# Strassen sums and centring by accumulating transfers in a Mish and convolution kernel

## The chip, the cores and the metric

The kernel runs on one core of one Trainium2 chip. The metric is the device time of one execution in microseconds. The chip executes a program on several engines that each work through a queue of their own in order: PE (matrix products), DVE (vector work), ACT (activations and copies), POOL (GpSimd) and SP, which only issues DMA transfers. Engines meet by semaphores: an instruction at the head of a queue waits until what it needs is done, and everything behind it in that queue waits too.

## The reference

The input `x` has 2048 rows of 640 channels. The output is `x + A(xn) + B(xn)`, where `xn` is `x` after a layer norm over the channels.

```python
xn = (x - mean(x)) / sqrt(var(x) + 1e-5)
h = xn @ w1 + b1                        # 640 -> 1728
act = h * tanh(softplus(h))             # Mish
B = act @ w2                            # 1728 -> 640
A = convolution of xn with K along the rows, + xn * D_skip
K = 2 * Re(sum_n C[d,n] * dt[d] * exp(dt[d] * A[d,n] * l))
```

For parameters as they are given here, `A` is computed as two running sums along the rows with coefficients per channel; a general path stands behind a flag that the kernel computes at run time and that isn't taken.

## The kernel before, in words

**Tiles.** Everything is transposed: channels lie on the 128 partitions, rows of `x` run along the free dimension. The 2048 rows are four blocks b of TB = 512. The 640 channels are KD = 5 tiles k, the 1728 hidden channels NF = 14 tiles f: thirteen of 128 and one, f = 8, of 64. Each operand of a product is split into a high and a low fp16 part, and each product is three: high by high, low by high and high by low. The first product of a tile, `mm1` (L773 in the profile), has 15 matmuls of 128x128x512; the second, `mm2` (L825), has 15 as well and adds into five accumulators ACC in PSUM. `mm2` runs LAG = 3 tiles behind `mm1`.

**Strassen.** In blocks 1 to 3 twelve of the fourteen tiles are taken in six pairs, PAIRS = (0, 2, 4, 6, 9, 11). For a pair, `mm1_pair` (L793) splits the problem two by two: two tiles f, two halves CA and CB of the 512 rows, and the four channel tiles 0 to 3 as two sets, {0, 2} and {1, 3}. It computes seven half-size products where plain work has eight. They are issued as five pieces called one, two, three_a, three_b and four, between which pieces of `mm2` are put. In between, small instructions move partial sums: `cV` and `cY` (ACT, L1029 and L1030) copy PV and PX out of PSUM bank TR, `z` and `w` (DVE, L1033 and L1037) add PVS to PY. Piece two waits for `cY`, three_a for `z`, four for `w`. The fifth channel tile is done plainly. Block 0 uses plain `mm1` for all tiles.

**Sums that Strassen needs.** Of the weights, four sums per pair, made once, in block 0 and block 1: `load_s` (L543) loads both tiles of a pair again from DRAM on SP's queue into two tiles of the pool "w", `sum_w` (L550, L552, L554, L556) makes the four sums of 128x256 on DVE, and `hi_s` (ACT, L568) and `lo_s` (DVE, L572) split them into fp16 parts, in three pieces of 256, 256 and 512 columns. The first sum takes the place of the even channel tiles of W1H[f+1] and W1L[f+1], which only block 0's plain product needs otherwise; the other three go to SWH[i] and SWL[i]. Of `x`, five differences per block, `sum_x` (L583), split by `hi_t` (L586) and `lo_t` (L590) into TH, TL, EH, EL.

**The layer norm of block c** for c = 1 to 3 is done while block c - 1 is computed: SP loads four tiles of rows (`lx`, L1086, pool "x" of two tiles), DVE makes their statistics (L597 to L599), POOL the reciprocal root and a copy of the means (`rstds`, L603, L604, L1193). PE transposes the eight columns (`spread`, L608), ACT copies them out of PSUM (`sr`, L612), SP writes them to DRAM (`sd`, L616) and loads them back, broadcast to all partitions, mean and rstd as two tiles (`spread_l`, L620). SP loads the transposed `x` (`load_xt`, L1189), and DVE subtracts the mean and multiplies by rstd, ten instructions of 128x512 (`norm_t`, L624). Then ACT and DVE split the result (`hi_x`, L535, and `lo_x`, L538), and `sum_x` follows. `spread` stands in PE's queue behind `mm1` of tile 7 in block 0, and in the fourth pair in blocks 1 and 2. Block 0 is normalised ahead of the rest, before its transposes.

**The convolution** of a block and channel tile (`ka` to `ke`, L709 to L729) needs two scans on DVE and ends with `ke`, which turns the tile XT[c][k] into the skip part of the output. POOL then adds `x` from DRAM into a copy of the accumulators with an accumulating DMA (`add_x`, L518), adds that into XT (`finish`, L739) and stores (`store`, L742). In the last block PE's last products and DVE's last sums alternate, and SP stores.

**What sets the order.** The function `whole` adds every piece of work to a planner, class Plan, with its engine, an assumed cost in microseconds, what it needs, which tile of a pool it takes and gives back, and for a DMA its kB. PE's order is fixed by the order of the `add` calls. For all other engines, and SP's and POOL's DMA issues, the planner walks through an assumed time and picks what is ready with the earliest due time; due times follow back from PE's order. `due` in `add` gives soft due times; `edge` spreads the convolution's over the run. The planner's order is the order of each engine's queue; at run time only semaphores count.

Of the kernel before, what the change touches and what calls it, by code (L numbers as in the profile page):

```python
# [20 lines left out]
P = 128  # L21
L = 2048
D = 640
# [10 lines left out]
HALF = 8  # L34
LAG = 3
# [201 lines left out]
def ffn_general(tc, x, xT, vec, w1, w2, out):  # L237
# [3 lines left out]
    with ExitStack() as es:  # L241
# [12 lines left out]
        for b in range(NB):  # L254
# [11 lines left out]
            for f, (n, o) in enumerate(zip(FC, FO)):  # L266
# [5 lines left out]
                for k in range(KD):  # L272
                    pe.matmul(h[:n], W1[:, k, :n], XN[:, k], start=k == 0, stop=k == KD - 1)
# [149 lines left out]
def body(ctx: ExitStack, tc: tile.TileContext, x, xT, logA, Aim, Cr, Ci, logdt, vec, w1, w1T, w2, w2T, out):  # L423
# [64 lines left out]
    XT, ACT, SM, NX = ({} for _ in range(4))  # L488
    NCHK = NF + 3 * KD
# [51 lines left out]
    def load_s(i, j):  # L541
        o = D * FO[PAIRS[i] + j]
        sp.dma_start(kf(pl["sw", i, j]), w1[o:o + D * P].rearrange("(p k f) -> p k f", p=P, k=KD))  # L543

    def sum_w(i, j):

        w = lambda n, m: kf(pl["sw", i, n])[:, 0:4].rearrange("p (q j) f -> p q j f", j=2)[:, :, m]
        t = lambda n: pl["ss", i, n // 2].rearrange("p (j q f) -> p j q f", j=2, q=2)[:, n % 2]
        if j == 0:
            v.tensor_tensor(t(0), w(1, 0), w(1, 1), op=OP.add)  # L550
        elif j == 1:
            v.tensor_tensor(t(1), t(0), w(0, 0), op=OP.subtract)  # L552
        elif j == 2:
            v.tensor_tensor(t(2), w(0, 0), w(1, 0), op=OP.subtract)  # L554
        else:
            v.tensor_tensor(t(3), w(0, 1), t(1), op=OP.subtract)  # L556

    def part_w(i, j):
        f = PAIRS[i] + 1
        t = pl["ss", i, j // 2].rearrange("p (j q f) -> p j q f", j=2, q=2)  # L560
        if j == 0:
            sh, sl = (w[f][:, 0:4].rearrange("p (q j) f -> p q j f", j=2)[:, :, 0] for w in (W1H, W1L))
            return sh, sl, t[:, 0]
        return (SWH[i][:, 0], SWL[i][:, 0], t[:, 1]) if j == 1 else (SWH[i][:, 1:3], SWL[i][:, 1:3], t)
# [12 lines left out]
    def sum_x(c, j):  # L577

        x = XT[c][:, 0:4].rearrange("p (q j) t -> p q j t", j=2)
        b11, b12, b21, b22 = (x[:, :, i, h] for i in range(2) for h in (CA, CB))  # L580
        p, q = ((b12, b11), (b22, j == 1 and stage(c, 0)), (b22, b12), (b21, j == 3 and stage(c, 1)),
                (XT[c][:, 4, CA], XT[c][:, 4, CB]))[j]
        v.tensor_tensor(stage(c, j), p, q, op=OP.subtract)  # L583

    def hi_t(c, j):
        a.activation(EH if j == 4 else TH[j], stage(c, j), AF.Copy, scale=SX)  # L586

    def lo_t(c, j):
        hi, lo = (EH, EL) if j == 4 else (TH[j], TL[j])
        v.scalar_tensor_tensor(lo, stage(c, j), SX, hi, op0=OP.mult, op1=OP.subtract)  # L590
# [27 lines left out]
    def spread_l(c):  # L618
        for j in range(2):
            sp.dma_start(pl["b", c][j], NX["sd"][j * NT:(j + 1) * NT].rearrange("(o i) p -> o (i p)", o=1).to_broadcast([P, TB]))  # L620

    def norm_t(c, k, j):
        z = XT[c][:, k]
        v.tensor_tensor(z, z, pl["b", c][j], op=(OP.subtract, OP.mult)[j])  # L624

# [118 lines left out]
    def bank(b, f):  # L744

        if b > 0:
# [3 lines left out]
    def mm1_part(f, kinds, c, start=False, stop=False, ks=range(KD)):  # L750
# [3 lines left out]
        for j, ((w, x), k) in enumerate(seq):  # L754
            pe.matmul(bank(0, f)[:, c], w[:, k], x[k][:, c], start=start and j == 0, stop=stop and j == len(seq) - 1)  # L755

    def mm1(b, f):
# [3 lines left out]
        hh, lh, hl = ([(h, w[f][:, k], x[k]) for k in range(KD)] for w, x in ((W1H, xh), (W1L, xh), (W1H, xl)))  # L761
# [13 lines left out]
    def mm1_pair(b, f):  # L775

        i = PAIRS.index(f)
        wh = [[W1H[f + j][:, k] for k in range(KD)] for j in range(2)]
        wl = [[W1L[f + j][:, k] for k in range(KD)] for j in range(2)]
# [133 lines left out]
    def whole():  # L913
# [8 lines left out]
        def chain(b, f, pre, drop=()):  # L922
# [7 lines left out]
            elif b > 0 and f in PAIRS:  # L930
# [52 lines left out]
        for f in range(3, NF):  # L983
            prev = {3: 0, 4: 1}.get(f, f - 2)
            add(("m1", 0, f), M, 15 * M5 if FC[f] == P else 1.85, mm1, 0, f,
                pre=[("hw1", f), ("ow1", f), ("v1", 0, prev), ("sg", 0, prev)] if f > 3 else [("v1", 0, prev), ("sg", 0, prev)])
            chain(0, f, [("m1", 0, f)])
            if f == 7:
                add(("spread", 1), M, 0.1, spread, pre=[("rs", 1)])
            for o in second(0, f - LAG, []):  # L990
                o()


        def vc(b):
            return ("vX", b - 1, PAIRS[-1]) if b > 1 else ("v1", 0, 2)

        for b in range(1, NB):
            for f in range(NF):
                n = (b, f)
                if f - 1 in PAIRS:  # L1000
# [3 lines left out]
                if f not in PAIRS:  # L1004
                    pb = before(b, f)
                    add(("m1", *n), M, 15 * M5 if FC[f] == P else 1.85, mm1, b, f,
                        pre=[("v1", b, f - 2), ("sg", b, f - 2)])
                    chain(b, f, [("m1", *n)])
                    for o in second(*g2, []):
# [3 lines left out]
                c = b  # L1013
                one, two, three_a, three_b, four = mm1_pair(b, f)
                p0 = (b, PAIRS[i - 1]) if i else (b - 1, PAIRS[-1])
                first = b == 1 and i == 0
                lastB = ("v1", 0, LAST) if first else ("v1", *before(b, f)) if f in (0, 9) else ("v1", *p0)
                lastC = ("v1", 0, LAST - 1) if first else ("v1", p0[0], p0[1] + 1)
                lastA = [("v1", 0, 2), ("sr", 1)] if first else [("cY", *p0), ("vX", *p0)]
                if (b, i) in ((1, 4), (2, 4), (3, 4)) and b < NB - 1:  # L1020
                    lastA.append(("sr", b + 1))
                if (b, i) == (NB - 1, NP - 1):
                    lastA.append(("oke",))
                SWD = lambda j: [("os", i, j)] if b == 1 else []
                TXD = lambda j: [("tl", b, j)]
                XLD = lambda ks: [("lo", b, k) for k in ks]
                A2, B2 = second(*g2, [9] if FC[g2[1]] == P else [6]), second(*h2, [3, 9] if FC[h2[1]] == P else [2, 6])
                add(("one", *n), M, 12 * M2, one, pre=lastA + SWD(0) + TXD(0) + XLD((0, 2)))
                add(("cV", *n), A, 0.36, lambda: a.copy(PVS, PV), pre=[("one", *n)] + ([] if first else [("w", *p0)]))  # L1029
                add(("cY", *n), A, 0.36, lambda: a.copy(PY, PX), pre=[("cV", *n), lastC])  # L1030
                A2[0]()
                add(("two", *n), M, 15 * M2, two, pre=[("cY", *n)] + SWD(1) + TXD(1) + XLD((1, 3, 4)))
                add(("z", *n), V, 0.38, lambda: v.tensor_tensor(PZ, PY, PVS, op=OP.add), pre=[("two", *n), lastB])  # L1033
# [7 lines left out]
                if i == NP - 2 and b == NB - 1:  # L1041
                    add(("oks",), M, 0.1, ok_sum, pre=[("ce", "last"), ("vX", *n)])
# [7 lines left out]
                chain(b, f + 1, [("four", *n), ("w", *n)])  # L1050

# [30 lines left out]
        for c in range(1, NB):  # L1082
            b = c - 1
            t0 = start(b, 0)
            for i in range(NT):
                add(("lx", c, i), S, 0.1, lambda c=c, i=i: sp.dma_start(pl["x", c, i], xr[c, i]),  # L1086
                    pre=[("st", c, i - 2)] if i > 1 else [], take=("x", ("x", c, i), 1), rel=t0, kb=327.0)
# [4 lines left out]
            add(("bc", c), S, 0.2, spread_l, c, pre=[("sd", c)], take=("b", ("b", c), 2 * KD), kb=512.0)  # L1092
# [260 lines left out]
```

## Time and profile before

| what | us |
|---|---|
| median of 3 runs (360.0 to 360.25) | 360.2 |
| the profiled execution | 359.29 |
| its span, first to last instruction | 357.5 |
| PE busy in the span | 350.6 |
| DVE busy | 311.1 |
| ACT busy | 296.3 |
| POOL busy | 50.4 |
| block 0's `mm1` and `mm2` behind the start, to the first piece of block 1 | 20.7 to 89.2 |
| block 1, 2, 3 begin at | 89.2, 174.1, 258.8 |

The profile is of one execution. Its times are from the span's start. A row of a group gives line, engine, operation, names and shapes, a count, the busy time, the mean duration in ns, and the idle time of that engine just before with what ended it. A row of the timeline gives start, duration and the instruction. A row of the waits says which engine waited for what: total, times, longest. A matmul's duration includes its way through the array; the pace is the distance from one start to the next.

### The profile page before, as it was taken

The page shows a single profiled execution, that of the slowest core. Times are in us where ns is not written, and L with a number is a line of the kernel's source. Part 1 is how long each engine was busy: PE and PEld are TensorE (multiplying, and loading weights), DVE is VectorE, ACT ScalarE, POOL GpSimd, SP SyncE. Part 2 cuts the span into 40 slices and gives each one's busy share as a digit, 9 for nine tenths or more (in the row PEclk, how much of TensorE's full clock was granted, in tenths as well). Part 3 has the DMA queues.
Part 4 walks back from the last instruction along what each step waited for, and adds up shares of the span by engine and source line. Part 5 has one row for each costly group of instructions (what it writes and reads, how often), then busy time and mean ns, then how long its engine had stood idle before and what let it go on. Part 6 is the DMA issues. An engine that isn't in the chain of part 4 may idle for free.

```text
span 357.5 us, 6018 instructions
## 1 busy us (share of the span) xinstructions
PE 350.6 (98%) x2167; PEld 211.5 (59%) x2167; DVE 311.1 (87%) x585; ACT 296.3 (83%) x614; POOL 50.4 (14%) x72
## 2 busy tenths in 40 slices
PE   7999999999999999999999999999999999999995
PEld 6754444444666665665566666566566666566543
DVE  5989989989998999999999986899997888775552
ACT  3599999978488799889989897989978989868740
POOL 2100020000013041000103343000003552000000
PEclk9999999999999999999999999999999999999999
DMA  7879975105109954911256973941111994201003
GB/s 238 279 240 296 337 247 174 73 1 183 39 21 194 335 165 127 296 24 39 64 179 128 202 181 91 278 170 35 33 35 20 166 232 89 55 0 31 0 16 141
DMA packets 26036, 48.75 MB, mean 136 GB/s; under 512 B 3576, under 2 KB 6928, under 8 KB 26000
## 3 DMA queue, kind: packets, MB, share of 16 engines
q1 hardware_dynamic: 19152, 34.21, 29.8%
q0 software_dynamic: 6240, 13.11, 17.8%
q10 hardware_dynamic: 608, 0.98, 0.8%
q8 instruction: 19, 0.31, 0.4%
q14 instruction: 17, 0.14, 0.2%
HBM read 39.10 MB, written 5.26 MB: 124 GB/s over the span
## 4 chain that ended last, share of the span: by engine, by line
PE 95%; DMA 1%; DVE 1%; SPq 0%; ACT 0%; issue 0%; DVEq 0%
PE acc L825 48%; PE h L793 18%; PE h L773 14%; PE tr L793 12%; DMA x<-in_A_u_dram 1%; PE h L755 1%; PE tr L755 1%; PE acc L1217 0%; PE acc L839 0%; PE acc L836 0%; PE acc L837 0%; DVE w1l L526 0%; DVE st L598 0%; SPq L1236 0%; DVE st L597 0%
## 5 line engine op out<-in xcount | busy, mean ns | idle before, releaser
L825 PE MATMUL acc<-hi,w2h 128*128 128x512 f16 x273 | 100.9, 379 | 0.0
L825 PE MATMUL acc<-hi,w2l 128*128 128x512 f16 (+1 forms) x265 | 99.7, 379 | 0.0
L825 PE MATMUL acc<-lo,w2h 128*128 128x512 f16 x253 | 93.3, 379 | 0.0
L825 PEld LDWEIGHTS <-w2h 128*128 128x128 f16 x526 | 51.2, 98 | 48.4 <-issue 1.3
L863 ACT ACTIVATE s<-h,cv 128x512 f32<-128x512 f32 (+1 forms) x51 | 30.9, 605 | 23.6 <-PE h L793 18.4
L793 PEld LDWEIGHTS <-w1h 128*128 128x128 f16 x432 | 42.3, 98 | 10.7
L887 DVE SCALAR_TENSOR_TENSOR A<-p,A 128x512 f32<-128x512 f32 (+1 forms) x56 | 38.2, 682 | 7.2 <-ACT p L882 7.0
L825 PEld LDWEIGHTS <-w2l 128*128 128x128 f16 x273 | 25.6, 98 | 30.7 <-issue 1.1
L872 ACT ACTIVATE p<-s,kc 128x512 f32<-128x512 f32 (+1 forms) x56 | 40.1, 715 | 0.5
L882 ACT ACTIVATE p<-p,kc 128x512 f32<-128x512 f32 (+1 forms) x56 | 40.0, 714 | 0.2
L877 ACT ACTIVATE p<-p,kc 128x512 f32<-128x512 f32 (+1 forms) x56 | 39.9, 713 | 0.2
L905 DVE SCALAR_TENSOR_TENSOR lo<-A,hi 128x512 f16<-128x512 f32 x52 | 35.3, 680 | 3.6 <-ACT hi L894 3.3
L867 DVE SCALAR_TENSOR_TENSOR A<-h,bs,s 128x512 f32<-128x512 f32 (+1 forms) x51 | 33.0, 647 | 6.2 <-ACT s L863 6.0
L894 ACT ACTIVATE hi<-A 128x512 f16<-128x512 f32 (+1 forms) x56 | 34.9, 624 | 3.6 <-DVE A L887 3.4
L518 POOL DMA_DIRECT2D r<-in_xT_dram x15 | 13.7, 1094 | 126.8 <-ACT r L736 60.3
L773 PEld LDWEIGHTS <-w1h 128*128 128x128 f16 (+1 forms) x174 | 15.3, 99 | 20.3 <-issue 3.3
L715 DVE TENSOR_TENSOR_SCAN g<-g,car,kc 128x512 f32<-128x512 f32 x20 | 25.6, 1278 | 1.1 <-ACT g L709 1.1
L793 PEld LDWEIGHTS <-w1l 128*128 128x128 f16 x216 | 21.1, 98 | 8.4 <-issue 0.3
L719 DVE TENSOR_TENSOR_SCAN g<-g,car,g 128x512 f32<-128x512 f32 x20 | 25.5, 1276 | 0.1
L793 PE MATMUL tr<-xh,w1h 128*128 128x256 f16 x90 | 24.5, 273 | 0.1
L793 PE MATMUL tr<-xl,w1h 128*128 128x256 f16 x90 | 24.5, 273 | 0.0
L793 PE MATMUL tr<-xh,w1l 128*128 128x256 f16 x90 | 24.5, 273 | 0.0
(174 smaller groups left out, 728.7 us busy)
## 6 DMA issues: line engine op xcount, KB each, us to landing
w<-in_w_dram SPq DMA_DIRECT2D x23, 320.0 KB, 4.7
w<-in_w2T_dram SPq DMA_DIRECT2D x15, 288.0 KB, 6.4
w<-in_B_w_dram SPq DMA_DIRECT2D x13, 320.0 KB, 3.5
w<-in_w1T_dram SPq DMA_DIRECT2D x13, 320.0 KB, 6.6
x<-in_A_u_dram SPq DMA_DIRECT2D x12, 320.0 KB, 5.0
xt<-in_xT_dram SPq DMA_DIRECT2D x15, 256.0 KB, 5.5
r<-in_xT_dram POOLq DMA_DIRECT2D x15, 256.0 KB, 6.0
xt<-r POOLq DMA_DIRECT2D x15, 256.0 KB, 4.1
```

The costliest lines, as they stand in the source:

```text
L715: v.tensor_tensor_scan(g1[:, 1:], g1[:, 1:], zero.to_broadcast([P, TB]), car[:, 1, k:k + 1], op0=OP.add, op1=OP.add)
L773: pe.matmul(o, w, x, start=(j == 0), stop=(j == len(order) - 1))
L793: pe.matmul(o, p, q, start=start and n == 1, stop=n == 3 * len(w), skip_group_check=True)
L825: pe.matmul(o, w, x, start=start, stop=stop)
L863: a.activation(pl["s", b, f][:n, c], src(b, f) if h is None else h, AF.Sigmoid, bias=cv[:n, f:f + 1], scale=1 / SH)
L867: v.scalar_tensor_tensor(pl["A", b, f][:n, c], src(b, f) if h is None else h, bs[:n, f:f + 1], pl["s", b, f][:n, c], op0=OP.add, op1=OP.mult)
L872: a.activation(pl["p", b, f][:n], pl["s", b, f][:n], AF.Arctan, bias=one[:n], scale=-1.0)
L877: a.activation(p, p, AF.Square, bias=pi4[:n], scale=2.0)
L882: a.activation(p, p, AF.Tanh, bias=mb[:n], scale=MG)
L887: v.scalar_tensor_tensor(A, pl["p", b, f][:n], MC, A, op0=OP.add, op1=OP.mult)
L894: a.activation(hi[:n], A, AF.Copy, scale=MA * SA / SH)
L905: v.scalar_tensor_tensor(lo, A, MA * SA / SH, hi[:n], op0=OP.mult, op1=OP.subtract)
```

## The change

The four sums of weights per pair and the subtraction of the mean are no longer made by DVE. For the weights, SP loads three pieces into a new tile of four slots (pool "y", two such tiles): w11 into slots 0 and 1, w00 into slot 2, w01 into slot 3, where the first figure is the tile of the pair and the second the set of channels. POOL issues a transfer that adds w10 from DRAM to slots 0, 1 and 2 at once, then one that adds w00 to slot 1, which must wait for the first to land. DVE adds slot 1 to slot 3. `hi_s` and `lo_s` take two pieces now, 256 and 768 columns. So that a set's channels lie next to each other, the host writes w1's channel tiles in the order KP = (0, 2, 1, 3, 4), and every product reads `w[:, KP[k]]`.

The sums are all additions, where two were differences; to make up for it, one difference of `x` and the copy `cY` change sign, and `z` is a multiply and a subtraction in one instruction.

For the mean, `rstds` writes -mean, only rstd is loaded back as a broadcast tile, and POOL issues three transfers per block that add -mean, broadcast from `sd` in DRAM, to the loaded XT: channel tiles {0, 2}, then {1, 3}, then 4. They wait for `load_xt` and for `sd`. DVE only multiplies.

Beside that: the loop over blocks is written so that pairs of block 0 from number EARLY on could be Strassen pairs too. EARLY is 6, which is the number of pairs. `spread` of block 1 stands behind `mm1` of tile 8 now. The pool "x" is gone (rows for statistics take tiles of "w"), "t" has three tiles instead of four, "b" one instead of two. `x0_sum` may run earlier, and `edge` is set later.

```diff
+KP = (0, 2, 1, 3, 4)
...
+    EARLY = 6
+    paired = lambda b, f: f in PAIRS and (b > 0 or PAIRS.index(f) >= EARLY)
...
-    pl.pool("x", tiles(row, "x", 2, [P, D]))
-    pl.pool("t", tiles(row, "t", 4, [P, TB]))
+    pl.pool("t", tiles(row, "t", 3, [P, TB]))
+    pl.pool("y", tiles(row, "y", 2, [P, 4, 2, P]))
...
-    pl.pool("b", [[row.tile([P, TB], F32, name=f"bc{j}") for j in range(2)]])
+    pl.pool("b", tiles(row, "bc", 1, [P, TB]))
...
+    def load_s(i):
+        y = pl["y", i]
+        for j, k, at, m in ((1, 1, 0, 2), (0, 0, 2, 1), (0, 1, 3, 1)):
+            sp.dma_start(y[:, at:at + m], parts(i, j, k).to_broadcast([P, m, 2, P]))
+
+    def sum_w(i, n):
+        y = pl["y", i]
+        if n < 2:
+            j, m = ((1, 3), (0, 1))[n]
+            at = 0 if n == 0 else 1
+            g.dma_start(y[:, at:at + m], parts(i, j, 0).to_broadcast([P, m, 2, P]), accum_op=OP.add)
         else:
-            v.tensor_tensor(t(3), w(0, 1), t(1), op=OP.subtract)
+            v.tensor_tensor(y[:, 3], y[:, 3], y[:, 1], op=OP.add)
...
+    def center(c, n):
+
+        z = XT[c][:, 4:5] if n == 2 else XT[c][:, 0:4].rearrange("p (q j) t -> p q j t", j=2)[:, :, n]
+        m = NX["sd"][0:NT].rearrange("(o q i) p -> o q (i p)", o=1, q=1)
+        g.dma_start(z, m.to_broadcast([P, 1 if n == 2 else 2, TB]), accum_op=OP.add)
+
+    def norm_t(c, k):
         z = XT[c][:, k]
-        v.tensor_tensor(z, z, pl["b", c][j], op=(OP.subtract, OP.mult)[j])
+        v.tensor_tensor(z, z, pl["b", c], op=OP.mult)
...
-            if f == 7:
-                add(("spread", 1), M, 0.1, spread, pre=[("rs", 1)])
...
+                    if (b, f) == (0, 8) and EARLY > 3:
+                        add(("spread", 1), M, 0.1, spread, pre=[("rs", 1)])
...
-                add(("cY", *n), A, 0.36, lambda: a.copy(PY, PX), pre=[("cV", *n), lastC])
+                add(("cY", *n), A, 0.36, lambda: a.activation(PY, PX, AF.Copy, scale=-1.0), pre=[("cV", *n), used[1]])
...
-                add(("z", *n), V, 0.38, lambda: v.tensor_tensor(PZ, PY, PVS, op=OP.add), pre=[("two", *n), lastB])
+                add(("z", *n), V, 0.38, lambda: v.scalar_tensor_tensor(PZ, PY, -1.0, PVS, op0=OP.mult, op1=OP.subtract), pre=[("two", *n), used[0]])
...
+            for n in range(3):
+                add(("ce", c, n), G, 1.0, center, c, n, pre=[("lxt", c), ("sd", c)], kb=(512.0, 512.0, 256.0)[n])
             for k in range(KD):
-                add(("n", c, k, 0), V, 0.62, norm_t, c, k, 0, pre=[("lxt", c), ("bc", c)], drop=[("b", c)])
-                add(("n", c, k, 1), V, 0.62, norm_t, c, k, 1, pre=[("n", c, k, 0)], drop=[("b", c)])
+                add(("n", c, k, 1), V, 0.62, norm_t, c, k, pre=[("ce", c, 2 if k == 4 else k % 2), ("bc", c)], drop=[("b", c)])
...
+            add(("ls", i), S, 0.1, load_s, i, pre=[("os", order[order.index(i) - 2], 1)] if order.index(i) > 1 else [], take=("y", ("y", i), 2), rel=start(0, 3) if early else max(start(0, 8), start(1, f) - 40), kb=512.0)
...
-            add(("x0s", k), V, 0.62, x0_sum, k, rel=start(0, 9))
-        edge = [start(1, 4), start(2, 0), start(2, 11), start(3, 5), start(3, 11)]
+            add(("x0s", k), V, 0.62, x0_sum, k, rel=pl.t["PE"])
+        edge = [start(1, 4), start(2, 2), start(3, 0), start(3, 4), start(3, 11)]
...
-        g.tensor_copy(NX["st"][:, 0], NX["mv"][:, :, 0])
+        g.tensor_scalar(NX["st"][:, 0], NX["mv"][:, :, 0], -1.0, None, op0=OP.mult)
...
-    w1, b1 = B_w1.reshape(KD, P, F).transpose(1, 0, 2), B_b1
+    w1, b1 = B_w1.reshape(KD, P, F)[list(KP)].transpose(1, 0, 2), B_b1
```

More of the change, by code (lines that the diff above doesn't have):

```diff
@@ L754, in mm1_part @@
         for j, ((w, x), k) in enumerate(seq):
-            pe.matmul(bank(0, f)[:, c], w[:, k], x[k][:, c], start=start and j == 0, stop=stop and j == len(seq) - 1)
+            pe.matmul(bank(0, f)[:, c], w[:, KP[k]], x[k][:, c], start=start and j == 0, stop=stop and j == len(seq) - 1)
     def mm1(b, f):
@@ L760, in mm1 @@
         xh, xl = XH[b % 2], XL[b % 2]
[L761 removed]
+        hh, lh, hl = ([(h, w[f][:, KP[k]], x[k]) for k in range(KD)] for w, x in ((W1H, xh), (W1L, xh), (W1H, xl)))
         if n < P:
@@ L982, in whole @@
             chain(0, f, [("m1", 0, f)])
[L983 to L987, printed above, removed]
-            if f == 7:
-                add(("spread", 1), M, 0.1, spread, pre=[("rs", 1)])
[L990 to L998, printed above, removed]
+        used = {0: ("v1", 0, 0), 1: ("v1", 0, 1)}
+        p0 = None
+        for b in range(NB):
+            for f in range(0 if b else 3, NF):
                 n = (b, f)
-                if f - 1 in PAIRS:
+                if paired(b, f - 1):
                     continue
@@ L1106, in whole @@
                     take=("t", ("ts", c, j), 2 if j < 2 else 1), drop=[("ts", c, j - 1 - (j == 3))] if j in (1, 3) else [])
-                war = [((("one", "two", "three_a", "four", "four")[j]), c - 1, PAIRS[-1])] if c > 1 else []
+                war = [((("one", "two", "three_a", "four", "four")[j]), c - 1, PAIRS[-1])] if paired(c - 1, PAIRS[-1]) and c else []
                 add(("th", c, j), A, 0.54 if j < 4 else 0.36, hi_t, c, j, pre=[("tx", c, j)] + war)
                 add(("tl", c, j), V, 0.62 if j < 4 else 0.38, lo_t, c, j, pre=[("th", c, j)], drop=[("ts", c, j)])
+        order = [*range(EARLY, NP), *range(EARLY)]
```

102 lines of the change are left out of this document (43 added, 59 removed).

## The prediction

> **What bounds the kernel now.** I read the page first, then the waits of PE, then busy time by stage. From the page, busy time and the chain that ended last:
>
> ```profile
> PE 350.6 (98%) x2167; PEld 211.5 (59%) x2167; DVE 311.1 (87%) x585; ACT 296.3 (83%) x614; POOL 50.4 (14%) x72
> ...
> PE 95%; DMA 1%; DVE 1%; SPq 0%; ACT 0%; issue 0%; DVEq 0%
> ```
>
> A busy PE need not be PE at its pace, so I ask where it waits. The waits of PE, all of them:
>
> ```profile
> PE tr L1231 <- POOL car L464: 1.4, 1, 1.4
> PE acc L1217 <- DVE x L1201: 0.6, 2, 0.3
> PE h L755 <- ACT w1h L522: 0.2, 1, 0.2
> ```
>
> All three lines belong to the first 15 us (fill, transposes of block 0, first products). The windows by stage (PE, PEld, DVE, ACT, POOL, then clock, DMA share, GB/s), for the end of block 0 and for block 1:
>
> ```profile
> 60.00:89.20 29.20, 29.20 (x138) 12.95 (x136) 28.20 (x49) 25.48 (x53) 0.00 (x0) 1.00 0.32 106
> 89.20:174.20 85.00, 84.94 (x559) 53.73 (x558) 81.99 (x176) 72.39 (x154) 13.53 (x17) 1.00 0.49 133
> ```
>
> PE is busy for 29.20 of 29.20 us and for 84.94 of 85.00, at clock 1.00. That it also runs at its pace is seen in one row of the chain in order of time (start, length, what):
>
> ```profile
> 55.09 3.24 PE acc L825 x15
> ```
>
> 15 products of 128x512 take 3.24 us, 0.216 us each, and such rows follow each other without a hole. I looked through the PE rows for a hole behind this and found one that isn't a missing record, at 158.9:
>
> ```profile
> 158.67 0.38 PE L825 MATMUL acc<-hi,w2l 128*128 128x512 f16 x1
> 159.11 0.27 PE L793 MATMUL tr<-xh,w1h 128*128 128x256 f16 x1
> ...
> 158.69 0.37 ACT L1030 COPY h<-tr 128x256 f32<-128x256 f32 x1
> ```
>
> The next product was due 0.22 us after 158.67 and came after 0.44: it waited for the copy of PX, which ended at 159.06. So **0.22 us** is all that PE lost after the start. At the end PE is again the last to finish, and DVE with the last store follow it:
>
> ```profile
> 352.88 0.27 PE L847 MATMUL h<-lo,w2h 128*128 128x256 f16 x1
> 353.19 0.42 DVE L910 SCALAR_TENSOR_TENSOR xt<-h,xt 128x256 f32<-128x256 f32 x1 [0.56 <-PE h L847]
> ```
>
> The bound is the number of matmul columns. DVE, at 82 of 85 us in block 1, is nearly full too, but nothing on PE waits for it.
>
> **The change part by part.** *PE.* EARLY is 6, the number of pairs, so no pair of block 0 becomes a Strassen pair: paired(0, f) is false for all f, bank() and the loop give block 0 the same plain products, and blocks 1 to 3 the same 54 half-width products per pair. KP only renames rows of the weights. PE's term of the sum is 0 us.
>
> *DVE and ACT.* The rows of what goes and what changes (count, busy us, mean ns):
>
> ```profile
> L624 DVE TENSOR_TENSOR xt<-xt,bc 128x512 f32<-128x512 f32 x30 | 19.7, 681 | 0.0
> ...
> L572 DVE SCALAR_TENSOR_TENSOR swl<-t,swh 128x512 f16<-128x512 f32 x6 | 4.0, 674 | 0.0
> ...
> L572 DVE SCALAR_TENSOR_TENSOR swl<-t,swh 128x256 f16<-128x256 f32 x6 | 2.5, 420 | 0.0
> ...
> L554 DVE TENSOR_TENSOR t<-w,w 128x256 f32<-128x256 f32 x6 | 2.5, 417 | 0.0
> L556 DVE TENSOR_TENSOR t<-w,t 128x256 f32<-128x256 f32 x6 | 2.5, 416 | 0.0
> ...
> L550 DVE TENSOR_TENSOR t<-w 128x256 f32<-128x256 f32 x6 | 2.5, 411 | 0.0
> ```
>
> Half of L624 (15 subtractions) goes: -9.85 us. Of the four groups of six sums of weights three go and an addition like them stays: -7.5. The low halves of 256 and 512 become one of 768: 256 more columns cost 674 - 420 = 254 ns, so 928 instead of 1094, six times, -1.0. Two instructions change their form; the nearest rows, the second of each pair being the new form at the same size:
>
> ```profile
> L1033 DVE TENSOR_TENSOR h<-h,pvs 128x256 f32<-128x256 f32 x18 | 7.7, 428 | 6.5 <-PE h L793 6.3
> L867 DVE SCALAR_TENSOR_TENSOR A<-h,bs,s 128x256 f32<-128x256 f32 x18 | 8.5, 472 | 1.8 <-ACT s L863 1.7
> ...
> L1030 ACT COPY h<-tr 128x256 f32<-128x256 f32 x18 | 6.8, 376 | 0.0
> ...
> L863 ACT ACTIVATE s<-tr,cv 128x256 f32<-128x256 f32 x18 | 8.3, 460 | 1.7 <-PE tr L793 1.7
> ...
> L568 ACT ACTIVATE swh<-t 128x512 f16<-128x512 f32 x6 | 3.7, 620 | 1.4 <-DVE t L556 1.4
> ...
> L568 ACT ACTIVATE swh<-t 128x256 f16<-128x256 f32 x6 | 2.4, 407 | 0.0
> ```
>
> z (L1033) costs 0 to 44 ns more, 18 times: at most +0.8. DVE in all: -9.85 - 7.5 - 1.0 + 0.8 = **-17.5 us** of 311.1. ACT: hs as one of 768 is 833 ns instead of 1027, six times -1.2; the copy of PX as an activation is 0 to 84 ns longer, 18 times up to +1.5; in all about 0. Everything that leaves DVE lay beside a PE that didn't wait for it, so it is worth **0** at the end. The longer copy is the one edit on PE's heels: where PE waited for it by 0.22 us, it waits up to 84 ns more, and if a second pair is as tight, as much again. I take +0.1 us (0 to +0.2).
>
> *POOL and DMA.* 21 transfers come: two per pair of weights, three for each of blocks 1 to 3. Their issue and landing, by the nearest rows (the first of the last three is SP's load of weights):
>
> ```profile
> L518 POOL DMA_DIRECT2D r<-in_xT_dram x15 | 13.7, 1094 | 126.8 <-ACT r L736 60.3 <-DVE r L734 58.5 <-ACT s L863 5.9
> ...
> L739 POOL DMA_DIRECT2D xt<-r x15 | 13.3, 885 | 39.8 <-DVE xt L729 26.2 <-DVE A L867 9.4 <-DMA r<-in_xT_dram 2.0
> ...
> w<-in_w_dram SPq DMA_DIRECT2D x23, 320.0 KB, 4.7
> ...
> r<-in_xT_dram POOLq DMA_DIRECT2D x15, 256.0 KB, 6.0
> ...
> xt<-in_xT_dram POOLq DMA_DIRECT2D x5, 256.0 KB, 3.7
> ```
>
> These have 128 rows each. The new ones have up to 384 pieces, so one issue lies between 0.885 us (if pieces don't count) and 3 x 1.094 = 3.3; I take 1.1 to 2.2. In all 39 times 128 pieces, at most 43 us on a POOL that is busy 50.4 of 357: it hides in POOL's idle time. DMA has room (share 0.32 before block 1, 0.49 in it). SP's queue gets three loads per pair for two, and each third pair's load waits for one of two buffers; behind it on SP stand the rows of x for the next statistics.
>
> The Trainium skill (page "SBUF — State Buffer", section "SBUF: two separate sides") speaks against moving work here: GpSimd writes the descriptors of its own DMAs, and while VectorE holds the port they share, such a DMA stands still; the page's example goes from about 0.6 to 3.1 us. By it, three issues would take about 6 us more ahead of block 1, an estimate from that page, which the spare worked out below still covers. The trace doesn't show the effect: 885 and 1094 ns are means beside a DVE that was busy 82 of 85 us.
>
> *The path to block 1* is the step that moves most. Its rows:
>
> ```profile
> 49.73 0.27 PE L608 MATMUL tr<-ident,st_row 128*8 128x128 f32 x1
> ...
> 53.81 0.24 ACT L612 COPY sr<-tr 8x128 f32<-8x128 f32 x1
> ...
> 54.11 0.35 SPq L616 DMA_DIRECT2D sd<-sr  x1
> 56.69 1.12 SPq L620 DMA_DIRECT2D bc<-sd  x2
> ...
> 60.84 0.68 DVE L624 TENSOR_TENSOR xt<-xt,bc 128x512 f32<-128x512 f32 x1
> ...
> 72.01 0.68 DVE L590 SCALAR_TENSOR_TENSOR tl<-t,th 128x512 f16<-128x512 f32 x1
> ...
> 89.24 0.27 PE L793 MATMUL tr<-th,w1h 128*128 128x256 f16 x1
> ```
>
> The spread moves from behind m1(0,7) to behind m1(0,8), whose end is the 55.09 above: +5.4 us. From the spread to the first use of sd it is 56.69 - 49.73 = 7.0, so the first transfer of -mean is issued at 62.1. It lands 3.7 to 6.0 later, plus up to 1.1 for its second half: first product with rstd at 65.8 to 69.2, against 60.84. The second transfer, which the sums of x also need, is 1.1 to 2.2 behind. From the first norm to tl it was 72.01 - 60.84 = 11.2, with five subtractions between that now go. So tl stands at 77 to 82.6, and PE wants it at 89.24: spare **6 to 12 us**. Cost 0, because block 0's products cover it. The later blocks' spread keeps its place on PE, and DVE has 3.4 us less for each.
>
> **Sum.** The profiled execution took 359.29, of which 357.5 is the span; the median is 360.2, so 0.9 us above it. 0 (PE) + 0 (DVE, POOL) + 0.1 (copy) on 360.2 gives **360.3 us**; own range 359.8 to 360.9 (the one hole closed, and small new ones).
>
> **The rivals.** *A, slower: the path to block 1 is late on POOL.* POOL runs in order. If the transfers of -mean stand behind a weight's second accumulate, that one waits for its first (6.0) and the first for its load (4.7): up to 10.7 us. It decides from 6 us of delay on; price 0.7 to 4.7, so 361 to 365. For it: all of this is new on POOL in just that stretch. Against: POOL was empty there (0.00 in the window to 89.20), and the first weights are asked for earlier than the mean. Chance 0.22.
>
> *B, slower: the statistics are late for the spread, which stands in PE's own queue.*
>
> ```profile
> 127.57 0.65 POOL L1193 COPY st_row<-mv 128x4 f32<-128x4 f32 x1
> ...
> 135.14 0.27 PE L608 MATMUL tr<-ident,st_row 128*8 128x128 f32 x1
> ...
> POOL out_dram L742 <- DMA xt<-r: 35.3, 10, 7.6
> ```
>
> Spare 135.14 - 128.22 = 6.9 us. A POOL wait for a landing took up to 7.6; with an issue of 1.1 that is 8.7, a stall of 1.8, and two in front of the statistics give up to 8, once or twice in the run: 361 to 368, nearest 362. Against: most of the weights' sums can be done before. Chance 0.16.
>
> *C, faster: DVE was the real limit.* If PE's rows only look full and DVE paces them, the 17.5 us come off: 342.7, or anything down to it. Against it stand 0.216 us per product and the single hole of 0.22. The Trainium skill (page "Perfetto Trace Analysis", section "Identifying the Most-Contended Engine") gives this rule: matmul busy time misleads, LDWEIGHTS busy share is the measure; by that PE is at 59% and DVE at 87% the most contended. The rows above disagree, by the pace. Chance 0.05.
>
> *D, the change doesn't do what it says* (DVE no less busy, since sums wait elsewhere) gives 360.2 too and is inside the forecast.
>
> **How the numbers follow.** Forecast 0.57, A 0.22, B 0.16, C 0.05. A measurement of this kernel can tell about 0.2%, 0.7 us, from no change: below 359.5 counts as faster, above 360.9 as slower. Faster 0.05, same 0.57, slower 0.38. For 8 in 10 the range needs 0.23 of the 0.38 on the slow side, the lower half of A and B: 359.8 to 363.0.
>
> **What would show it.** Right: PE's waits still hold only the first 15 us, block 1 still takes 85.0 us, DVE's busy time falls to about 293.6, POOL's rises by 19 to 43 with its idle time ended by DMA landings. Wrong: a wait of PE on tl or xl at the start of block 1 (A), a PE idle in front of the spread (B), a shorter block 1 to 3 (C), or a PE wait on the copy of PX in many pairs, which would put my +0.1 at up to 1.5.

## The result and the profile after

The changed kernel takes **409.45 us** (median of 5 runs, 409.05 to 409.99) against 360.0 in the same comparison (359.51 to 360.25): ratio 1.1378, 95% interval 1.1362 to 1.1394. I had predicted 360.3, in a range of 359.8 to 363.0. The profiled execution has a span of 407.8 us, 50.3 more than before.

From the page of the kernel after, busy time, the granted clock in 40 slices and the chain that ended last:

```profile
PE 364.5 (89%) x2167; PEld 216.5 (53%) x2167; DVE 297.1 (73%) x546; ACT 296.8 (73%) x608; POOL 72.4 (18%) x93
...
PEclk9999999878898989995999999995999999999999
...
PE 50%; DMA 16%; issue 13%; ACT 11%; DVE 5%; POOL 3%; SPq 0%; ACTq 0%; POOLq 0%; DVEq 0%
```

PE runs the same 2167 matmuls. It is idle for 407.8 - 364.5 = 43.3 us, against 357.5 - 350.6 = 6.9 before: 36.4 us. The other 364.5 - 350.6 = 13.9 us of the 50.3 are products that took longer, where the clock row shows 5 to 8. The chain, 95% PE before, is half PE now; of the rest, 29% are transfers and "issue" (time in which an engine waited for nothing that the profile shows), 16% ACT and DVE. Block 1 begins at 100.82 here (89.24 before) and block 2 at 212.81. By stage (columns as before), the rows for the end of block 0 and for block 1:

```profile
60.00:100.82 40.82, 33.35 (x141) 14.05 (x139) 24.55 (x43) 24.06 (x50) 8.62 (x8) 0.87 0.56 98
100.82:212.81 111.99, 92.22 (x558) 56.73 (x556) 77.93 (x159) 75.92 (x155) 22.09 (x26) 0.91 0.59 141
```

27.2 of PE's 43.3 idle us lie in these two. In block 1 PE, DVE and ACT are busy for a smaller share than before, DVE for 78 us of 112 where it was 82 of 85: none of the three is overloaded, they wait. The longest of PE's waits behind the start:

```profile
PE h L800 <- DVE h L1028: 13.8, 2, 7.3
PE tr L800 <- ACT h L1025: 8.1, 4, 3.6
PE h L780 <- DVE A L874: 7.5, 2, 5.4
PE acc L832 <- DVE lo L912: 4.6, 3, 2.5
```

None of these names something that the change adds. L1028 is `z`, L1025 `cY`, L874 and L912 the Mish of a tile already computed: short instructions of old work, whose input PE had long given. So one asks what stood in front of them. The longest waits of DVE, ACT and POOL that end with a transfer of the change or with "issue", and one more ahead of L628:

```profile
DVE xt L632 <- DMA xt<-sd: 24.5, 5, 6.0
```

```profile
ACT w1h L571 <- DMA y<-in_w_dram: 20.4, 5, 7.1
```

```profile
POOL y L560 <- DMA y<-in_w_dram: 32.7, 5, 10.3
POOL xt L628 <- issue: 26.0, 4, 10.2
...
POOL xt L628 <- DMA w<-in_w1T_dram: 9.7, 1, 9.7
...
POOL y L560 <- issue: 7.9, 3, 3.5
```

L632 is DVE's multiply by rstd, L571 ACT's high half of the weight sums, L628 POOL's transfers of -mean, L560 those of the weights. The 9.7 us are put down to a load of weights that a transfer of -mean doesn't need: in the code it waits for the transposed `x`, whose loads were issued at 124 us, and for `sd`. They belong with the waits for issue, as the first experiment shows. One hole of PE, 7.25 us in block 1, followed back through the timelines of PE, DVE and POOL:

```profile
180.23 0.38 PE L832 MATMUL acc<-hi,w2l 128*128 128x512 f16 x1
187.86 0.37 PE L800 MATMUL h<-th,swh 128*128 128x256 f16 x1 [7.25 <-DVE h L1028]
```

```profile
184.97 2.50 DVE L632 TENSOR_TENSOR xt<-xt,bc 128x512 f32<-128x512 f32 x4 [4.35 <-DMA xt<-sd]
187.38 0.42 DVE L1028 SCALAR_TENSOR_TENSOR h<-h,pvs 128x256 f32<-128x256 f32 x1
```

```profile
178.08 2.13 POOL L628 DMA_DIRECT2D xt<-sd  x2 [9.66 <-DMA w<-in_w1T_dram]
```

Read upwards: POOL issues the last two transfers of -mean for block **2** at 178; DVE has had its multiply for block 2 at the head of its queue since 180.6; `z`, which block **1** needs now, stands behind it; PE stands behind `z`. Work of the next block holds up the current one. The same in block 0, where DVE's multiplies for block 1 stand in front of the Mish of tiles that PE is at:

```profile
65.26 1.25 POOL L628 DMA_DIRECT2D xt<-sd  x1 [6.49 <-issue]
71.60 1.21 POOL L628 DMA_DIRECT2D xt<-sd  x1 [5.09 <-issue]
```

```profile
77.75 1.29 DVE L632 TENSOR_TENSOR xt<-xt,bc 128x512 f32<-128x512 f32 x2 [4.38 <-DMA xt<-sd]
...
81.37 0.74 DVE L874 SCALAR_TENSOR_TENSOR A<-h,bs,s 128x512 f32<-128x512 f32 x1
...
82.63 0.68 DVE L593 SCALAR_TENSOR_TENSOR tl<-t,th 128x512 f16<-128x512 f32 x1
```

```profile
82.17 2.29 PE L780 MATMUL h<-xh,w1h 128*128 128x512 f16 x5 [5.44 <-DVE A L874]
```

The first `tl` is made at 82.63, at the end of the 77 to 82.6 that I had worked out, and before block 1 needs it. PE was held up all the same, in block 0.

### The profile page after: what moved, and what is told of

It is laid out like the page before. It is cut to its first block, busy times and chain, and to the rows that moved or that the text cites. A ratio compares the mean times of both kernels' runs of the same rounds, so it can differ in the third digit from the quotient of the medians.

```text
span 407.8 us, 6063 instructions
## 1 busy us (share of the span) xinstructions
PE 364.5 (89%) x2167; PEld 216.5 (53%) x2167; DVE 297.1 (73%) x546; ACT 296.8 (73%) x608; POOL 72.4 (18%) x93
## 4 chain that ended last, share of the span: by engine, by line
PE 50%; DMA 16%; issue 13%; ACT 11%; DVE 5%; POOL 3%; SPq 0%; ACTq 0%; POOLq 0%; DVEq 0%
PE acc L832 24%; PE h L800 14%; DMA y<-in_w_dram 8%; PE tr L800 7%; DMA xt<-sd 3%; PE h L780 3%; DMA w<-in_w_dram 2%; DMA w<-in_w1T_dram 2%; ACT p L879 2%; ACT s L870 2%; ACT p L884 1%; ACT p L889 1%; ACT w1h L525 1%; POOL xt L628 1%; ACT w2h L532 1%
## 5 line engine op out<-in xcount | busy, mean ns | idle before, releaser
L800 PEld LDWEIGHTS <-w1h 128*128 128x128 f16 x432 | 43.4, 100 | 11.8
L870 ACT ACTIVATE s<-h,cv 128x512 f32<-128x512 f32 (+1 forms) x51 | 30.7, 602 | 18.1 <-PE h L800 15.6
L912 DVE SCALAR_TENSOR_TENSOR lo<-A,hi 128x512 f16<-128x512 f32 x52 | 35.6, 685 | 6.9 <-ACT hi L901 6.7
L874 DVE SCALAR_TENSOR_TENSOR A<-h,bs,s 128x512 f32<-128x512 f32 (+1 forms) x51 | 33.2, 651 | 8.8 <-ACT s L870 8.4
L800 PE MATMUL h<-th,swh 128*128 128x256 f16 x72 | 20.8, 288 | 13.8 <-DVE h L1028 13.8
L780 PE MATMUL h<-xh,w1h 128*128 128x512 f16 x85 | 25.8, 408 | 7.5 <-DVE A L874 7.5
L780 PEld LDWEIGHTS <-w1h 128*128 128x128 f16 (+1 forms) x174 | 16.2, 104 | 30.4 <-issue 15.5
L632 DVE TENSOR_TENSOR xt<-xt,bc 128x512 f32<-128x512 f32 x15 | 9.7, 687 | 30.8 <-DMA xt<-sd 24.5
L800 PEld LDWEIGHTS <-swh 128*128 128x128 f16 x216 | 22.5, 104 | 5.8
```

The source lines that it names most:

```text
L780: pe.matmul(o, w, x, start=(j == 0), stop=(j == len(order) - 1))
L800: pe.matmul(o, p, q, start=start and n == 1, stop=n == 3 * len(w), skip_group_check=True)
L870: a.activation(pl["s", b, f][:n, c], src(b, f) if h is None else h, AF.Sigmoid, bias=cv[:n, f:f + 1], scale=1 / SH)
L874: v.scalar_tensor_tensor(pl["A", b, f][:n, c], src(b, f) if h is None else h, bs[:n, f:f + 1], pl["s", b, f][:n, c], op0=OP.add, op1=OP.mult)
L912: v.scalar_tensor_tensor(lo, A, MA * SA / SH, hi[:n], op0=OP.mult, op1=OP.subtract)
```

## The experiments

Two theories stood after this. *Queue heads* (Q): the loss is what stands behind waiting instructions, because the planner puts them at the head of DVE's and ACT's queues at a time when it believes their data landed; it reckons about 4 us per transfer. *Space* (R, and S in the text of the run with the small space at the end; S in the first run's text is the rival that the Trainium skill's page gives): POOL's "issue" waits come from the 1024 bytes of `dynamic_dma_scratch_size`, which I take by its name to be the room for the descriptors of POOL's own DMAs, and which an accumulating transfer fills so far that the next has to wait. The rival (L): accumulating transfers burden the DMA or the engines as such, so that no order would help. All times below are medians; the kernel before, run beside them, gave 359.7 to 360.1. Line numbers shift by a few from kernel to kernel.

**Twice the space.** The kernel after with one number changed:

```diff
-_BACC = {"dynamic_dma_scratch_size": 1024}
+_BACC = {"dynamic_dma_scratch_size": 2048}
```

> The changed kernel with twice the space for descriptors of GpSimd's transfers (2048 bytes instead of 1024), nothing else. Theory R (POOL can't issue an accumulate before an earlier one has drained, because that space is full): POOL's idle time put down to issue, 42 us in the changed kernel, falls below 8 us, the transfers of -mean are issued 1.3 us apart instead of 6, and the time falls to 375 to 395. Theory S (the descriptors are written slowly beside a busy DVE, as the Trainium skill's page SBUF, State Buffer, section SBUF: two separate sides, would have it): space changes nothing, 405 to 412.

389.65 us, ratio 1.0834 (1.0804 to 1.0864). The groups of the two kinds of transfer on POOL:

```profile
L560 POOL DMA_DIRECT2D y<-in_w_dram x12 | 13.9, 1156 | 55.5 <-DMA y<-in_w_dram 49.5 <-DVE A L894 6.0
L628 POOL DMA_DIRECT2D xt<-sd x9 | 10.9, 1642 | 0.8 <-issue 0.8
```

POOL's wait of 26.0 us ahead of L628 has become 0.8, that ahead of L560 none, and the 9.7 us put down to a load of weights are gone too: the space was what it waited for. It is worth 20 us; 30 remain, since the same transfers still land late for whoever stands at a queue's head (PE waited 8.9 us for `z`).

**Each half of the change alone.** First the kernel before with the mean subtracted by POOL's transfers, all else as before:

```diff
+            for n in range(3):
+                add(("cm", c, n), G, 1.0, center, c, n, pre=[("lxt", c), ("sd", c)], kb=(512.0, 512.0, 256.0)[n])
             for k in range(KD):
-                add(("n", c, k, 0), V, 0.62, norm_t, c, k, 0, pre=[("lxt", c), ("bc", c)], drop=[("b", c)])
...
```

> The kernel before with the mean alone changed: three accumulating transfers of -mean per block on POOL, weights summed by DVE as before, spread and due times as before. Theory Q (what is lost is lost behind instructions at the head of DVE's and ACT's queues that wait for an accumulate, while work for PE stands behind them): PE waits for z or v1 near the starts of blocks 1 to 3, some 7 us each, 375 to 385. If the weights are the whole cause: 359 to 362.

385.91 us, ratio 1.0735 (1.0697 to 1.0772), a little above what was expected. The waits of PE, DVE and POOL:

```profile
PE h L797 <- DVE h L1037: 14.9, 2, 8.2
```

```profile
DVE xt L628 <- DMA xt<-sd: 22.8, 5, 5.7
```

```profile
POOL xt L624 <- issue: 28.1, 3, 10.9
```

Then the kernel after with the mean back on DVE, as an addition of -mean (two broadcast tiles again, and to make room two tiles in "t" for three):

```diff
-            for n in range(3):
-                add(("ce", c, n), G, 1.0, center, c, n, pre=[("lxt", c), ("sd", c)], kb=(512.0, 512.0, 256.0)[n])
             for k in range(KD):
...
+                add(("n", c, k, 0), V, 0.62, norm_t, c, k, 0, pre=[("lxt", c), ("bc", c)], drop=[("b", c)])
...
```

> The changed kernel with the mean back on DVE (two broadcast tiles, ten instructions per block), so the weights' sums alone go through POOL; the pool t has two tiles to make room. Theory Q: ACT's hi of a weight sum waits at the head of its queue, 375 to 390, with PE waits in block 1 alone and none at the start of blocks 2 and 3. If the mean is the whole cause: 359 to 362.

377.89 us, ratio 1.0507 (1.0465 to 1.0549). Here it is ACT that waits, with `cY` behind it:

```profile
PE tr L801 <- ACT h L1026: 10.4, 4, 4.9
```

```profile
ACT w1h L571 <- DMA y<-in_w_dram: 15.4, 5, 5.6
```

The two losses, 25.8 and 17.8 us, add up to 43.7 of the 49.5 (each against the kernel before beside it): two separate cases of one mechanism. With the mean alone it is DVE that waits for transfers, with the weights alone mostly ACT (15.4 us; DVE 7.2).

**The later spread.** The kernel after with the statistics' transposes back behind tile 7, as a check on the one step that was moved on PE:

```diff
-                    if (b, f) == (0, 8) and EARLY > 3:
+                    if (b, f) == (0, 7) and EARLY > 3:
```

> The changed kernel with the spread of block 1 behind the first product of tile 7 again, as before the change; nothing else. My prediction put this move at 5.4 us of the path to block 1. Theory Q: the waits at the heads of the queues depend on how the planner's time differs from the chip's, and both move together, so little changes: 403 to 411. If the later spread is itself a cause: 395 to 403, with the holes of block 0 gone.

408.04 us, ratio 1.1348 (1.1329 to 1.1367). It isn't the spread.

**The planner told the truth.** Nothing but assumed times in the planner: the new transfers land 8 us after their issue, are wanted 8 us (not 4) ahead of their users, and the larger hold POOL for 7:

```diff
-                    wait = 4.0 if q["kb"] else self.GAP[q["eng"]]
+                    wait = 8.0 if q["kb"] and q["name"][0] in ("ss", "ce") else 4.0 if q["kb"] else self.GAP[q["eng"]]
...
+                if o["name"][0] in ("ss", "ce"):
+                    end = max(end, t + 8.0)
+                    if o["kb"] > 300:
+                        self.t[e] = t + 7.0
```

> The changed kernel whose planner is told what the transfers take: an accumulate for weights or mean lands 8 us after its issue (it reckoned 3 to 5), POOL stands still for 7 us after the larger ones, and what feeds them is due 4 us earlier. Same instructions, another order in the queues. Theory Q: DVE and ACT find other work ahead of the waiting instruction, 360 to 370. Rival L (the path through the transfers is too long for its place whatever the order): 395 or more.

378.88 us, ratio 1.0535 (1.0507 to 1.0564), outside both ranges, nearer to Q's: 31 us are gone with the same transfers and the same space, while POOL's waits for issue stayed (38.4 us ahead of the transfers of -mean alone). With both cures, 8 us and 2048 bytes, without the 7 us on POOL:

> The changed kernel with both mends: 2048 bytes of descriptor space, and a planner that reckons 8 us from an accumulate's issue to its landing (POOL is not held, since the space is there). If space and order are the whole cause (R and Q): 360 to 364, PE's holes after the start under 3 us in all. If the transfers themselves or their traffic cost (contention, or L, a path too long for its place): 370 or more.

371.8 us, ratio 1.0318 (1.0249 to 1.0388). Too slow for R and Q as I had them, and in the range that I had given to contention and L. The timelines of POOL and DVE show what is left:

```profile
139.14 3.38 POOL L631 DMA_DIRECT2D xt<-sd  x3 [2.29 <-DMA sd<-sr]
```

```profile
151.29 0.69 DVE L635 TENSOR_TENSOR xt<-xt,bc 128x512 f32<-128x512 f32 x1 [4.54 <-DMA xt<-sd]
...
153.94 0.43 DVE L1031 SCALAR_TENSOR_TENSOR h<-h,pvs 128x256 f32<-128x256 f32 x1
```

With space for all three, they are issued back to back. The trace's landing row for these lines:

```profile
DMA to landing us min/median/max: 7.6/12.8/17.0
```

In the kernel after, where the three of a block were issued over some 12 us, it was 4.0/6.9/11.1. So 8 us was still not the truth, and what was left is again DVE's L635 in front of `z`. If that is all, a later reckoning removes it; if it is the transfers as such, it doesn't. That gave the decisive run: 17 us for the transfers of -mean, 8 for the sums of weights, 2048 bytes.

```diff
+LATE = {"ss": 8.0, "ce": 17.0}
...
-                    wait = 4.0 if q["kb"] else self.GAP[q["eng"]]
+                    wait = LATE.get(q["name"][0], 4.0) if q["kb"] else self.GAP[q["eng"]]
...
-                end = max(end, self.dma + 1.9)
+                end = max(end, self.dma + 1.9, t + LATE.get(o["name"][0], 0.0))
```

> The kernel after with 2048 bytes of descriptor space, in which the planner reckons 17 us from issue to landing for the three transfers that subtract the mean (as measured with all three issued together) and 8 us for the weight sums. Theory Q (what is lost is lost by instructions that stand at the head of DVE's and ACT's queues before their data have landed): 359.5 to 364 us, the holes in PE in front of blocks 2 and 3 (3 to 5 us each in the run with 8 us for all) gone, DVE's wait for xt from these transfers below 8 us in sum. Rival L (the accumulating transfers slow the other transfers or engines whatever the order): 369 us or more, with holes of the same size elsewhere.

**361.53 us**, ratio 1.0043 (1.0029 to 1.0057). Of the page, and of DVE's and POOL's timelines:

```profile
PE 350.2 (97%) x2167; PEld 210.6 (59%) x2167; DVE 295.6 (82%) x546; ACT 298.2 (83%) x608; POOL 74.4 (21%) x93
...
PE 92%; ACT 2%; DVE 2%; DMA 1%; issue 1%; ACTq 0%
```

```profile
153.68 0.41 DVE L1033 TENSOR_TENSOR h<-h,pvs 128x256 f32<-128x256 f32 x1
...
155.04 1.28 DVE L633 TENSOR_TENSOR xt<-xt,bc 128x512 f32<-128x512 f32 x2
```

```profile
139.46 3.37 POOL L629 DMA_DIRECT2D xt<-sd  x3 [2.01 <-DMA sd<-sr]
```

```profile
DMA to landing us min/median/max: 7.0/12.6/17.6
```

The transfers are issued together and land as late as in the run before, 12.6 us in the middle. But the multiply begins 15.6 us behind the issue, without a wait, and the small sums of the current block stand in front of it. The issue is where it was in the run before (139.14 there), so it is the multiply's place in the queue that moved. Of PE's waits on DVE behind the start 0.3 us is left, and PE's busy time is that of before. L falls as the cause of the loss: the accumulating transfers moved the same bytes. The run is still 1.7 us above the kernel before, clear of noise. In the profiled execution PE waits 1.7 us more for DVE's `x` in its first 13 us (2.3 against 0.6), ahead of all these transfers; whether that is so in the other runs isn't shown.

**The late reckoning with the small space.** The same with 1024 bytes:

> g1_late17 with the 1024 bytes of descriptor space of the change (nothing else differs). If the late reckoning alone is enough (Q): 361 to 364 us, POOL waiting some 40 us of issue again but nobody late for it. If both are needed (S with Q): 366 to 380, with holes in PE in the stretch of block 0, where POOL's waits for space push the weight sums of the first pairs behind their 8 us, and none at blocks 2 and 3, where 17 us cover the three transfers even when POOL issues them 10 us apart.

379.48 us, ratio 1.0568 (1.0524 to 1.0611): both are needed. The waits of PE, DVE and POOL:

```profile
PE tr L801 <- ACT h L1026: 6.3, 1, 6.3
PE h L801 <- DVE h L1033: 5.0, 1, 5.0
```

```profile
DVE y L563 <- DMA y<-in_w_dram: 18.5, 4, 8.6
...
DVE xt L633 <- DMA xt<-sd: 1.1, 1, 1.1
```

```profile
POOL y L561 <- issue: 17.9, 5, 5.4
POOL xt L629 <- issue: 11.7, 2, 6.9
```

As expected, 17 us cover the mean even so (1.1 us), while the weight sums, reckoned at 8, come late where POOL waits for space. But the two large holes lie in block 1, at 102 and 140 us, and not in block 0 as I had expected. Ahead of the second, DVE stood still for 5.5 us for a weight sum, with `w` (L1033 here) behind it. DVE's longest wait for a sum, 8.6 us, ended at 81.4, well ahead of the first hole; what links the two isn't shown. With the first two kernels that makes a table of four, us:

| reckoned landing | 1024 bytes | 2048 bytes |
|---|---|---|
| as in the change | 409.45 | 389.65 |
| 8 and 17 us | 379.48 | 361.53 |

Space is worth 20 or 18 us, the reckoning 30 or 28: they nearly add. The reckoning moves the users of a transfer back in their queues and what feeds it forward; for the weights the runs don't separate the two.

**Half the space for the kernel before.** If POOL's accumulating transfers wait for space, the fifteen of `finish` and fifteen of `add_x` should also come near to it; I thought they were too small and far apart.

```diff
-_BACC = {"dynamic_dma_scratch_size": 1024}
+_BACC = {"dynamic_dma_scratch_size": 512}
```

> The kernel before with half the descriptor space for GpSimd's transfers (512 bytes), nothing else. R: its accumulates of 256 KB, issued 1 us apart before, now wait for each other on POOL (issue time above 10 us in its waits). But nothing of PE's work stands behind a wait for them on DVE or ACT, so the time stays within 359.5 to 361.5.

369.02 us, ratio 1.0265 (1.0211 to 1.0319): a miss. The waits of PE and POOL:

```profile
PE tr L608 <- POOL st_row L1193: 5.8, 2, 4.9
```

```profile
POOL xt L739 <- issue: 15.1, 5, 3.5
```

In the kernel before, POOL's waits for issue are 2.6 us in all. With half the space they are 19.7, the statistics stand behind them on POOL, and the spread, in PE's own queue, behind the statistics. That is my rival B in another kernel, with a wait for issue where I had priced one for a landing. It also shows the space from the other side.

**Using what DVE has spare.** DVE is 15.5 us less busy in the last good version, so two more pairs of block 0 could be Strassen pairs (EARLY = 4), 1.2 us less for PE (30 products at 0.216 us per pair against 54 half ones at 0.109), on the version with 17 us, and on that without the mean's transfers; and the latter without more pairs:

```diff
-    EARLY = 6
+    EARLY = 4
```

> As g1_late17, and two more chunk pairs of block 0 as Strassen pairs (EARLY = 4 for 6), which takes 2 x 0.58 = 1.2 us of PE's products away but needs two pairs' weight sums earlier. Q: 358.3 to 364, at or below g1 if its sums land in time; if two pairs more in block 0's stretch, where 20 us of holes lay after the change, are too many, 365 to 372 with the holes between 60 and 150 us. L: above g1.

> The weight sums alone (the mean subtracted by DVE as before), with 2048 bytes of space and 8 us told to the planner. Q: 359.5 to 362, no hole over 1.5 us from 92 to 153 us, where the weights alone left 14 us of them. L: 368 or more.

> As g3_weights17, with two more Strassen pairs in block 0 (EARLY = 4). Q: g3 less 1.2 us of products if the sums are in time (358.3 to 361), which would be below the kernel before; otherwise holes in block 0 of 1 to 6 us in sum, 361 to 366. L: 368 or more.

Measured: 368.77 us (ratio 1.0243, 1.0216 to 1.027), 360.27 (1.0007, 0.9998 to 1.0017) and 366.05 (1.0178, 1.0161 to 1.0195). The weight sums alone, with space and true times, cost nothing: the 17.8 us of loss are gone. Two more pairs cost more than they give. With the weights alone PE's idle time rises from 8.5 to 12.7 us, in holes of up to 1.4 us over the whole run, with only 0.25 us in block 0, where I had expected them; and PE's busy time rises by 0.7 us where I had expected 1.2 less. DVE has 8.4 us more to do (313.4 against 305.0). Whether that is the cause isn't shown. With the mean's transfers the holes lie at 77 us (3.1 us) and behind 296 us; I had expected them between 60 and 150. That 368.77 is above the run with 17 us is also what L says, and no run here separates the two. No version here beats the kernel before.

## Why the prediction was wrong

*Right.* PE's term of 0: the products are the same and, where nothing is late, take the same 350 us. What leaves DVE is worth nothing: with 15.5 us less for DVE the time is 361.53. That also settles rival C, and with it the rule of the Trainium skill (page "Perfetto Trace Analysis", section "Identifying the Most-Contended Engine"): the engine that it names most contended was not the bound. Most pieces were priced well: `cY` and `z` are as long as before, the issue of a new transfer took 1.16 to 1.23 us where I said 1.1 to 2.2, POOL's busy time rose by 22.0 us (19 to 43). DVE's fell by 14.0, where I said 17.5.

*Luck.* The path to block 1 ended at 82.63, and I had said 77 to 82.6. But its steps were not mine: the first transfer of -mean was issued at 65.26 where I had 62.1, and the second 6.3 us behind it, where I had 1.1 to 2.2, because POOL waited for issue.

*Wrong: "Cost 0, because block 0's products cover it".* I priced the new waits by the deadline of the last thing on the path, `tl`, and there were indeed no late ones. But a product covers a wait only while PE has products, and block 0's come through the same DVE and ACT queues in which the new waits stand. I named for POOL what is behind a waiting instruction; I never asked it of DVE (L632, with `z` and the Mish of the current tiles behind it) or of ACT (L571, with `cY` and the Mish's functions behind it). Five waits on DVE, 24.5 us in all, and five on ACT, 20.4 in all, are where it was paid; with later reckoned landings and the space they are gone, and so is the loss. The rivals A and B had the wrong place. (B's upper end was also summed too low: two waits with their issues make 2 x 8.7 - 6.9 = 10.5 us, not 8.) For blocks 2 and 3 I had only that the spread keeps its place and DVE has less to do; the two holes in front of `z`, 13.8 us, come from the multiplies for just these blocks. The trace of before could have told: DVE is busy for 82 of 85 us, so what stands behind a wait is work that is due, and PE takes up `z` 0.6 to 1.3 us after its end in each of the 18 pairs. The tightest of them, `z` on DVE and piece three_a on PE:

```profile
119.81 0.41 DVE L1033 TENSOR_TENSOR h<-h,pvs 128x256 f32<-128x256 f32 x1
...
120.81 0.27 PE L793 MATMUL h<-th,swh 128*128 128x256 f16 x1
```

*Wrong: "it hides in POOL's idle time".* The time of issue does. What I left out is that issue itself can wait: 43.6 us are put down to issue in the kernel after (2.6 before), worth about 20. The code has the number that decides it, the 1024 bytes, and most of the new transfers have two or three times the 128 pieces of those before; that it is the pieces which fill the space is likely, not shown.

*Not in the sum at all:* PE's slower products after its longer holes, 13.9 us of the 50.3.

*The rule that spoke against the change* (the Trainium skill, page "SBUF — State Buffer", section "SBUF: two separate sides": GpSimd can't write descriptors while VectorE, in a 2-port mode, holds the shared ports) was right in its direction by luck, since issue was part of the trouble. The runs show another cause: with twice the space the waits are gone while DVE is as busy as ever (297.4 us against 297.1).

## What to carry to other kernels

Where an instruction gets a new wait, look at its own queue first: the price is what stands behind it there, and not only the deadline of its result. A schedule made ahead is only as good as the times it assumes; when work moves to a slower route, measure its landing, alone and in company, and tell the planner before judging the move. And before giving POOL larger transfers, look at the space reserved for them: in these runs a wait put down to "issue" ahead of POOL's DMAs was its sign.

## What the runs showed of the hardware

**POOL's DMA issue waits when `dynamic_dma_scratch_size` is small.** Doubling it in the kernel after took the waits put down to issue from 43.6 us to 1.7, halving it in the kernel before took them from 2.6 to 19.7. That it holds descriptors I take from its name. How much of it one transfer takes was not measured.

**Accumulating transfers land late, and later in company.** The transfers of -mean, 512 and 256 KB, landed 4.0 to 11.1 us after issue when a block's three were issued over some 12 us, and 7.0 to 17.6 when two or all three of them were issued back to back.

**The clock falls after a hole of two microseconds.** PE's timeline in the kernel after, right behind a hole of 2.02 us; then the windows from there on (PE, PEld, DVE, ACT, POOL, clock, DMA share, GB/s):

```profile
92.66 2.25 PE L780 MATMUL h<-xh,w1h 128*128 128x512 f16 x5 [2.02 <-DVE A L874]
94.70 1.96 PE L780 MATMUL h<-xl,w1h 128*128 128x512 f16 x5
96.50 1.24 PE L780 MATMUL h<-xh,w1l 128*128 128x512 f16 x5
97.58 0.38 PE L832 MATMUL acc<-hi,w2h 128*128 128x512 f16 x1
```

```profile
92.60:96.00 3.40, 3.34 (x9) 1.17 (x9) 3.40 (x7) 3.18 (x11) 1.30 (x1) 0.52 0.31 94
96.00:100.00 4.00, 4.00 (x20) 1.85 (x19) 4.00 (x9) 4.00 (x10) 0.00 (x1) 0.98 0.68 98
```

For 3.4 us the granted clock is 0.52. The first five products take 2.04 us from start to start (92.66 to 94.70), the next 1.80, and from 96.50 on 1.08, as before the holes. So a hole of 2.02 us cost 3.7. Behind the first 20 us of the kernels here there are 31 holes of 2 us and more, and in the 3.4 us behind each of them the mean clock was 0.50 to 0.72; behind 15 of the 19 holes of 0.9 to 1.8 us it stayed at 1.00. The Trainium skill (page "TensorE: Matmul & The Clock Gate", section "Part 1: The HAM clock gate") has the array at half clock after an idle window of about 3.4 us, and back after as much work. The way back agrees with the trace; the way down came after a shorter hole here, so here less than a whole such window without work was enough.
